# One core, a gated mix of a state-space convolution and segmented attention: reciprocals, softmax sums, joined rows and results moved by fewer, larger DMAs, partial results stored to the output and read back there

## The chip, the cores and the metric

The kernel runs on one core of a Trainium2 chip. The metric is the device time of one execution in microseconds; the chip is not shared with another kernel. A core has a matrix engine (PE, with its weight loads PEld), a vector engine (DVE), a scalar engine (ACT), a general one (POOL), and SyncE (SP), which computes nothing and issues nearly all DMAs of this kernel. The transfers themselves are carried by the core's 16 DMA engines.

## The reference

The input is `x` of 2048 rows and 448 columns. Two branches are computed from it and mixed by a gate, one number per row:

```
g   = sigmoid((x * gate_w).sum(-1))
a   = conv(x, K) + x * D_skip            # K from a diagonal state-space model, by FFT of length 4096
q,k,v = x@wq, x@wk, x@wv                 # 16 heads of 28, four segments of 512 rows
for s in range(4):
    p     = softmax(q_s k_s^T * scale + causal mask)
    a_dot = p @ v_s
    a_mem = (phi(q_s) @ M) / (phi(q_s) @ z + 1e-6)    # M, z: sums over the segments before
    o_s   = sig(beta) * a_mem + (1 - sig(beta)) * a_dot
b   = o @ wo
out = g * a + (1 - g) * b
```

## The kernel before, in words

Everything runs in float32. The first half of the program (to about 440 us) builds the convolution kernel `K` with exponentials and sines, projects `x` to queries, keys and values, and stores what the second half needs in DRAM tiles. The second half interleaves two streams: the attention of 16 units (4 segments by 4 groups of 4 heads; head j of a group holds the partitions 32j to 32j+31) and the convolution by FFT. The order of the work in it is a string, `PLAN`, in which each letter is one step; `run` maps letters to steps. Within an engine the work then stands as the string gives it; DMAs on SP stand in the order in which the scheduler placed them, and SP works through them in that order: a DMA that has to wait holds back those behind it.

The change touches these steps.

- `inverse`, called by `norm` (softmax sums) and by `recall` (sums of the memory branch). The sums of one segment, 4 groups by 512 rows for each of 4 heads, lie as a tile of 128 partitions by 64 columns, 32 partitions for each head. DVE takes the reciprocal `rc` and splits it in two parts `rs[:, 0]` and `rs[:, 1]`, and SP brings each part back as rows of `r8`, one row (one partition) per head: a row of 2048 numbers is gathered from 32 partitions of 64. PE then spreads such rows over the partitions by a matmul with `sel` (`ps_m<-r,sel` in the profile).
- `norm` first brings the sums out of row 28 of each head's 32 partitions of `pvs` into that 128 by 64 tile, `dn`. `norm` and `recall` run once for each of segments 0 to 2 (letter `e`); the last segment divides on PE and DVE instead (`divide`, letter `d`).
- The end of each segment writes `TB`, a DRAM tile of 2048 by 448: for segments 0 to 2 the finished attention part and the skip part, for segment 3 the skip part alone.
- `finish` is the end of the convolution, in 8 steps `wc`. Letter `l` is its `load` (transformed rows `bt`, 896 KB), letter `j` its `join` (the rows of `TB` that belong to the step, into the tile `rest`, of which there are six), letter `z` its `last`: matmuls with `fc` into `py`, a multiply-add of `py` by the gate into `rest` on DVE, and the stores. A tile of step `wc` holds the rows 32n + 16h + 2wc and the next one, for n from 0 to 63 and h of 0 or 1; h picks the half of the partitions. Its rows of segments 0 to 2 (n under 48) are results and go to `out`; those of segment 3 (n from 48) still lack the attention part and go to a DRAM tile `YD`.
- `last_end` reads `YD` back as four tiles `yd`, adds the attention part of segment 3 on DVE, and stores them to `out`, two by SP and two by ACT.

Of the kernel before, what the change touches and what calls it, by code (L numbers as in the profile page):

```python
# [12 lines left out]
F32 = mybir.dt.float32  # L13
# [10 lines left out]
D = 448  # L24
# [3 lines left out]
SEG = 512  # L28
# [442 lines left out]
class Feed:  # L471
# [9 lines left out]
    def step(self):  # L481
        tag = next(self.steps, None)
        self.count += 1
        self.done, self.held = tag is None, tag == "pe"
        cost = tag if isinstance(tag, float) else 0.0
        self.ends = cost < 0
        return abs(cost)
# [165 lines left out]
def finish(nc, k, fp):  # L653

    bv = k.BB.rearrange("k r (h w) d -> (k r) h w d", h=2)
    ov = k.out.rearrange("(n h w) d -> h n w d", h=2, w=16)
    tv = k.TB.rearrange("(n h w) d -> h n w d", h=2, w=16)  # L660
    yv = k.YD.rearrange("(n h w) d -> h n w d", h=2, w=16)
    bts, rest = {}, {}

    def load(wc):
        bts[wc] = fp.tile([128, 2, 2, D], F32, tag="bt", name="bt", bufs=5)
        k.dma(bts[wc], bv[:, :, 2 * wc : 2 * wc + 2])

    def join(wc):
        rest[wc] = fp.tile([128, 2, D], F32, tag="rest", name="rest", bufs=6)
        for h in range(2):  # L670
            k.dma(rest[wc][64 * h : 64 * h + 64], tv[h, :, 2 * wc : 2 * wc + 2])

    def last(wc):
        ws = slice(2 * wc, 2 * wc + 2)
        py = k.ps(("c", "mx")[wc % 2])
        for w in range(2):
            for h in range(2):
                k.mm(
                    py[64 * h : 64 * h + 64, w, :D], k.fc, bts[wc][:, h, w],
                    start=True, stop=True, tile_position=(0, 64 * h),  # L680
                )
        yo = rest.pop(wc)
        for w in range(2):
            i = 2 * wc + w
            k.dve.scalar_tensor_tensor(yo[:, w], py[:, w, :D], k.gt2[:, i : i + 1], yo[:, w], ALU.mult, ALU.add)
        for h in range(2):
            k.dma(yv[h, :, ws], yo[64 * h + 48 : 64 * h + 64])
        for h in range(2):
            k.dma(ov[h, :48, ws], yo[64 * h : 64 * h + 48])

    return load, join, last


# [278 lines left out]
def attend(nc, k, ap):  # L972
# [121 lines left out]
    def inverse(x, rows, dst):  # L1094


        rc = ap.tile([128, 64], F32, tag="rc", name="rc", bufs=2)
        rs = ap.tile([128, 2, 64], F32R, tag="rs", name="rs", bufs=2)
        v.reciprocal(rc, x)
        v.tensor_copy(rs[:, 0], rc)  # L1100
        v.tensor_tensor(rs[:, 1], rc, rs[:, 0], ALU.subtract)
        for b in range(2):
            for j in range(4):
                o = rows + 4 * b + j
                k.dma(
                    dst[o : o + 1].rearrange("o h (i f) -> o (h i) f", f=64).bitcast(F32),
                    rs[32 * j : 32 * j + 32, b].bitcast(F32),
                )

    am, r8 = {}, {}  # L1110

    def recall(s):

        dn = ap.tile([128, 64], F32, tag="dm", name="dm", bufs=1)
        k.ldma(dn, k.DM[s - 1].rearrange("j h (i f) -> (j h i) f", f=64))
        yield
        v.tensor_scalar(dn, dn, 1e-6, None, ALU.add)
        inverse(dn, 32, r8[s - 1])
        yield
        am[s] = ap.tile([128, 4, SEG], F32, tag="am", name="am", bufs=1)  # L1120
        k.ldma(am[s], k.AM[:, :, s - 1].rearrange("h p q -> p h q"))
        yield
        for hg in range(4):
            pb = k.ps("m")
            k.mm(pb, k.sel[32:40], r8[s - 1][32:40, hg], start=True, stop=True)
            v.scalar_tensor_tensor(am[s][:, hg], am[s][:, hg], k.gh[:, hg : hg + 1], pb, ALU.mult, ALU.mult)
            yield

    def norm(s):

        pvs = pvss[s]
        dn = ap.tile([128, 64], F32, tag="dn", name="dn", bufs=1)
        for j in range(4):
            k.dma(
                dn[32 * j : 32 * j + 32],
                pvs[32 * j + 28 : 32 * j + 29].rearrange("o h q -> o (h q)").rearrange("o (i f) -> o i f", f=64),
            )
        r8[s] = ap.tile([40, 4, SEG], F32R, tag="r8", name="r8", bufs=1)
        yield
        inverse(dn, 0, r8[s])  # L1140
        yield
        for hg in range(4):
            o = pvs[:, hg]
            pb = k.ps("m")
            k.mm(pb, k.sel[0:8], r8[s][0:8, hg], start=True, stop=True)
            v.scalar_tensor_tensor(o, o, k.omg[:, hg : hg + 1], pb, ALU.mult, ALU.mult)
            if s > 0:
                v.tensor_tensor(o, o, am[s][:, hg], ALU.add)
            yield
# [30 lines left out]
    def out_mm(s, t, po, hgs):  # L1180
        for hg in hgs:
            k.mm(
                po, pvss[s][:, hg, 128 * t : 128 * t + 128], wo[:, hg],
                start=(hg == 0), stop=(hg == 3),
            )
# [32 lines left out]
    def divide(hg):  # L1218

        o = pvss[3][:, hg]  # L1220
        pb = k.ps("m")
        k.mm(pb, k.den, o, start=True, stop=True)
        rc = ap.tile([128, SEG], F32, tag="jk", name="rcb", bufs=2)
        x = None
        for h in range(2):
            c = slice(256 * h, 256 * h + 256)
            with k.issue_after(x.ins) if x else ExitStack():
                v.reciprocal(rc[:, c], pb[:, c])
            v.scalar_tensor_tensor(o[:, c], o[:, c], k.omg[:, hg : hg + 1], rc[:, c], ALU.mult, ALU.mult)
            x = v.tensor_tensor(o[:, c], o[:, c], am[3][:, hg, c], ALU.add)  # L1230

    def last_end(step, vals):

        s = 3
        yds, pos = [], []
        for t in range(4):
            yd = ap.tile([128, D], F32, tag="xt", name="yd", bufs=4)
            k.dma(yd, k.YD[128 * t : 128 * t + 128])
            yds.append(yd)
        for t in ("w", "mx"):  # L1240
            pt = k.ps(t)
            pos += [pt[:, 0, :D], pt[:, 1, :D]]

        def project(h, hgs):
            for t in (2 * h, 2 * h + 1):
                out_mm(s, t, pos[t], hgs)

        project(0, range(2))
        step(vals)
        project(0, [2])  # L1250
        divide(3)
        project(1, range(2))
        for h in range(2):
            project(h, [2, 3] if h else [3])
            for t in (2 * h, 2 * h + 1):
                po, yd, i = pos[t], yds[t], 12 + t
                v.scalar_tensor_tensor(yd, po, k.ogt[:, i : i + 1], yd, ALU.mult, ALU.add)
                (k.dma, k.adma)[t % 2](k.out[128 * i : 128 * i + 128], yd)

    k.load_wo = load_wo  # L1260
    k.load, k.maxima, k.weigh, k.values, k.seg_end = load, maxima, weigh, values, seg_end
    k.divide, k.last_end, k.skip_last = divide, last_end, skip_last


def second_half(nc, k, ap, tp, fp, fin):
# [55 lines left out]
    def run(c):  # L1321
# [20 lines left out]
        elif c == "v":  # L1342
            step(vals)
        elif c == "q":
            k.twin = False
            k.load(n)
        elif c == "e":
            ends.append(k.seg_end(n))
        elif c == "s":
            while ends and not step(ends[0]):  # L1350
                ends.pop(0)
        elif c == "d":
            k.divide(n)
        elif c == "c":
            step(cv)
        elif c == "C":
            for _ in cv:
                pass
        elif c == "f":
            late = finish(nc, k, fin())  # L1360
        elif c == "k":
            if n == 0:
                skips = k.skip_last()
            else:
                step(skips)
        elif c == "o":
            k.load_wo()
        elif c in "ljz":
            late["ljz".index(c)](n)
# [24 lines left out]
def gated_mix(ctx, tc, k):  # L1394
# [102 lines left out]
    dr = ctx.enter_context(tc.tile_pool(name="dr", bufs=1, space=DRAM))  # L1497
# [11 lines left out]
    k.dr = dr  # L1509
    k.GD = dr.tile([L], F32, name="GD")  # L1510
    k.TB = dr.tile([L, D], F32, name="TB")
    k.YD = dr.tile([SEG, D], F32, name="YD")

    def const(name, ap, shape, dt=F32):
        t = cp.tile(shape, dt, name=name)
# [61 lines left out]
    with ExitStack() as st:  # L1577
# [25 lines left out]
        with ExitStack() as s2:  # L1603
# [5 lines left out]
            n = next(params)  # L1609
            k.ct = gp.tile([128, 2, 512], BF16, name="ct")  # L1610
            constants()
            while n is not None:
# [10 lines left out]
                n = next(params, None)  # L1623
# [68 lines left out]
```

## Time and profile before

| | |
|---|---|
| median of 3 runs | 797.93 us (796.94 to 803.42) |
| the profiled execution's own time | 796.75 us |
| its span, first to last instruction | 795.0 us |
| mean granted PE clock | 0.957 |
| busy share PE / DVE / ACT / POOL | 87% / 73% / 63% / 20% |
| DMA packets, bytes | 96146, 158.70 MB |

A row of the chain of waits has a start and a duration in us and what the chain went through: an engine's work on a tile with its line, a DMA from its issue to its landing (`DMA r<-rs`), or SP's issuing of DMAs (`SPq`). A row of a tile's view has the shortest, median and longest duration in ns, and the first and last start. A row of the table by stretches has the stretch, the busy time of PE, PEld, DVE, ACT and POOL with the count of instructions, the granted PE clock, the mean busy share of the 16 DMA engines, and the GB/s that they moved.

### The profile page before, as it was taken

The numbers are of one execution on the slowest core, as the hardware profiler recorded it, in microseconds if no ns is written. First come the engines' busy times: TensorE is split into PE (matmuls) and PEld (weight loads), VectorE is DVE, ScalarE is ACT, GpSimd is POOL, SyncE is SP. The second block draws the span as 40 slices with busy tenths as digits, with TensorE's granted clock in tenths as the row PEclk, the third lists the DMA queues.
The fourth block names the chain that finished last, engine by engine and source line by source line (L and its number), as shares of the span: only waits on it lengthen the run. The fifth ranks groups of instructions, "written<-read, shape, count | busy, mean of one in ns | idle before, by whom it ended". The sixth has DMA issues, their size and how long they took to land.

```text
span 795.0 us, 19029 instructions
## 1 busy us (share of the span) xinstructions
PE 689.2 (87%) x7609; PEld 382.2 (48%) x7640; DVE 582.7 (73%) x1154; ACT 501.9 (63%) x611; POOL 157.6 (20%) x193
## 2 busy tenths in 40 slices
PE   1676997999888998889997889899998999888987
PEld 1353565666545665447654434444444444444333
DVE  8979689869988798888876775658556757652673
ACT  4877689879998899988984225555345434511320
POOL 4405310111011101110111012232114113410110
PEclk9789999899999999999999999999998999969999
DMA  8628874136453344733357898895959596653973
GB/s 211 170 64 247 252 237 150 43 106 197 153 181 108 106 141 153 227 129 101 128 193 259 325 368 224 299 313 155 368 178 328 158 343 219 214 192 146 269 223 110
DMA packets 96146, 158.70 MB, mean 200 GB/s; under 512 B 25554, under 2 KB 63626, under 8 KB 96058
## 3 DMA queue, kind: packets, MB, share of 16 engines
q1 hardware_dynamic: 92106, 154.78, 59.9%
q10 hardware_dynamic: 3072, 1.84, 0.8%
q8 instruction: 60, 0.98, 0.5%
q0 software_dynamic: 880, 0.87, 0.4%
q14 instruction: 28, 0.23, 0.1%
HBM read 89.25 MB, written 60.24 MB: 188 GB/s over the span
## 4 chain that ended last, share of the span: by engine, by line
PE 51%; DVE 16%; ACT 13%; DMA 12%; issue 5%; SPq 3%; DVEq 0%; ACTq 0%
PE ps_m L1450 18%; PE ps_c L1450 6%; PE ps_w L1450 6%; PE ps_arg L1450 6%; ACT cs L1404 5%; PE ps_pv L1450 5%; PE ps_k L1450 5%; PE ps_mx L1450 4%; DVE Y L401 3%; DVE jk L1404 2%; PE ps_m L1453 2%; DVE cs L381 2%; DVE X L397 2%; DVE Y L402 2%; SPq L1466 1%
## 5 line engine op out<-in xcount | busy, mean ns | idle before, releaser
L1404 ACT ACTIVATE PT<-ps_w 128x1024 f32<-128x1024 f32 (+1 forms) x96 | 84.6, 881 | 127.5 <-PE ps_w L1450 124.3
L1404 DVE CUSTOM_DVE_ANT_0 jk<-ps_mx,mk 128x128 f32<-128x128 f32 (+3 forms) x242 | 106.9, 488 | 59.5 <-PE ps_mx L1450 55.5
L358 POOL TENSOR_TENSOR EX<-EX,cab 128x1024 f32<-128x1024 f32 x28 | 53.5, 1912 | 292.8 <-ACT EX L1404 209.1
L1404 ACT ACTIVATE cs<-ps_arg 128x1024 f32<-128x1024 f32 x97 | 94.5, 1023 | 11.0 <-DVE cs L381 10.8
L1071 POOL TENSOR_SCALAR_AFFINE_SELECT PT<-PT 128x256 f32<-128x256 f32 (+1 forms) x96 | 46.9, 488 | 235.2 <-ACT PT L1404 232.7
L1450 PE MATMUL ps_w<-qu,ku 32*128 32x512 f32 (+3 forms) x768 | 88.0, 347 | 3.0 <-ACT PT L1404 2.5
L1450 PE MATMUL ps_m<-xh,w 128*128 128x512 f32 x224 | 79.1, 413 | 1.5 <-DMA w<-WD 1.5
L1450 PE MATMUL ps_k<-Y,X 128*32 128x64 f32 x3584 | 62.9, 223 | 15.4 <-DVE Y L402 14.9
L397 DVE TENSOR_TENSOR X<-EX,cs 128x1024 f32<-128x1024 f32 x56 | 69.3, 1237 | 6.2 <-ACT cs L1404 5.6
L1450 PEld LDWEIGHTS ps_k<-Y,X 128*32 128x32 f32 x3584 | 53.6, 111 | 41.3 <-DVE Y L402 29.2
L1450 PEld LDWEIGHTS ps_w<-qu,ku 32*128 32x128 f32 x768 | 61.2, 189 | 23.6 <-ACT PT L1404 12.2
L401 DVE TENSOR_TENSOR Y<-EY,cs 128x1024 f32<-128x1024 f32 x56 | 70.1, 1252 | 0.0
L1404 ACT ACTIVATE cs<-cs,bhp 128x1024 f32<-128x1024 f32 x56 | 64.3, 1149 | 1.4
L1404 ACT ACTIVATE EY<-ps_arg 128x1024 f32<-128x1024 f32 x52 | 52.2, 1037 | 4.0 <-PE ps_arg L1450 3.8
L1450 PE MATMUL ps_mx<-ku,qu 32*128 32x128 f32 (+3 forms) x242 | 43.1, 389 | 12.2 <-DVE mx L1404 10.4
L1450 PEld LDWEIGHTS ps_m<-xh,w 128*128 128x128 f32 x224 | 42.0, 188 | 18.9 <-issue 8.9
L403 DVE SCALAR_TENSOR_TENSOR Y<-EY,cs 128x512 f32<-128x512 f32 x56 | 39.0, 696 | 15.3 <-ACT cs L1404 14.2
L1450 PE MATMUL ps_m<-xl,w 128*128 128x512 f32 x128 | 50.1, 391 | 0.0
L1450 PE MATMUL ps_arg<-ct,lh 64*128 64x512 bf16 x224 | 44.3, 382 | 4.7 <-ACT cs L1404 3.1
L1450 PEld LDWEIGHTS ps_mx<-ku,qu 32*128 32x128 f32 x242 | 21.0, 187 | 52.1 <-DVE mx L1404 29.7
L1450 PEld LDWEIGHTS <-lh 64*128 64x128 bf16 x392 | 22.0, 94 | 49.8 <-issue 35.1
L1450 PE MATMUL ps_m<-wo,pvs 128*128 128x448 f32 x96 | 40.9, 571 | 1.1 <-DVE tb L1404 1.1
(220 smaller groups left out, 1313.9 us busy)
## 6 DMA issues: line engine op xcount, KB each, us to landing
w<-WD SPq DMA_DIRECT2D x32, 448.0 KB
qu<-QD SPq DMA_DIRECT2D x16, 512.0 KB
ku<-KD SPq DMA_DIRECT2D x16, 512.0 KB
GU<-gs SPq DMA_DIRECT2D x32, 224.0 KB
GK<-gs SPq DMA_DIRECT2D x8, 896.0 KB
gk<-GK SPq DMA_DIRECT2D x16, 448.0 KB
gu<-GU SPq DMA_DIRECT2D x16, 448.0 KB
ks<-ks SPq DMA_DIRECT2D x32, 224.0 KB
```

Source lines behind the costliest of these rows:

```text
L358: nc.gpsimd.tensor_tensor(o, o, cab, ALU.mult)
L381: v.tensor_scalar(t[:, 0].rearrange("p w t c -> p t w c").bitcast(I32), pv.bitcast(I32), 0x7FFFFFFF, None, ALU.bitwise_and)
L397: v.tensor_tensor(X, ex, t[:, :, 0], ALU.mult)
L401: v.tensor_tensor(Y[:, :, :, :32], lo, y[:, :, :, ::-1], ALU.mult)
L402: v.tensor_tensor(Y[:, 0, :, 32:], ey[:, :, 32:], y[:, 0], ALU.mult)
L403: v.scalar_tensor_tensor(Y[:, 1, :, 32:], ey[:, :, 32:], -1.0, y[:, 1], ALU.mult, ALU.mult)
L1071: nc.gpsimd.affine_select(sl, sl, pat, ALU.is_ge, 0.0, base=0, channel_multiplier=-1)
L1404: x = op(*args, **kw)
L1450: tc.keep_in_program_order(nc.tensor.matmul(*args, **kw))
L1453: tc.keep_in_program_order(nc.tensor.transpose(*args))
L1466: return nc.sync.dma_start(*args)
```

## The change

The four DMAs of a part of the reciprocals become one, and so do the four that bring the sums out of `pvs`; the two halves of a join become one DMA, and the four stores of a `last` (two to `YD`, two to `out`) become one store of the whole tile to `out`, results and unfinished rows alike. `last_end` reads the unfinished rows from `out`. `YD` is gone. The bytes that move are the same.

```
     def join(wc):
         rest[wc] = fp.tile([128, 2, D], F32, tag="rest", name="rest", bufs=6)
-        for h in range(2):
-            k.dma(rest[wc][64 * h : 64 * h + 64], tv[h, :, 2 * wc : 2 * wc + 2])
+        k.dma(rest[wc], tv[:, :, 2 * wc : 2 * wc + 2])
...
     def last(wc):
...
-        for h in range(2):
-            k.dma(yv[h, :, ws], yo[64 * h + 48 : 64 * h + 64])
-        for h in range(2):
-            k.dma(ov[h, :48, ws], yo[64 * h : 64 * h + 48])
+        k.dma(ov[:, :, ws], yo)
...
     def inverse(x, rows, dst):
...
         for b in range(2):
-            for j in range(4):
-                o = rows + 4 * b + j
-                k.dma(
-                    dst[o : o + 1].rearrange("o h (i f) -> o (h i) f", f=64).bitcast(F32),
-                    rs[32 * j : 32 * j + 32, b].bitcast(F32),
-                )
+            o = rows + 4 * b
+            k.dma(
+                dst[o : o + 4].rearrange("o h (i f) -> o (h i) f", f=64).bitcast(F32),
+                rs[:, b].bitcast(F32),
+            )
...
     def norm(s):
...
-        for j in range(4):
-            k.dma(
-                dn[32 * j : 32 * j + 32],
-                pvs[32 * j + 28 : 32 * j + 29].rearrange("o h q -> o (h q)").rearrange("o (i f) -> o i f", f=64),
-            )
+        k.dma(
+            dn,
+            pvs.rearrange("(j e) h q -> j e (h q)", e=32)[:, 28].rearrange("j (i f) -> j i f", f=64),
+        )
...
     def last_end(step, vals):
...
-            k.dma(yd, k.YD[128 * t : 128 * t + 128])
+            k.dma(yd, k.out[128 * (12 + t) : 128 * (12 + t) + 128])
```

`tv` and `ov` are views of `TB` and `out` as `h n w d`, with h of length 2 outermost.

On SP, the end of segment 2 stands so before the change (a row has the line, the transfer as destination and source, the shape of the destination as the built program carries it, outermost length first, and the count of such DMAs in a row):

```order
L1466 DMA V<-VD 128x4x512
L1466 DMA dn<-pvs 32x1x64 x4
L1466 DMA BB<-bs 128x2x448 x2
L1466 DMA r_8596<-rs 1x32x64 x16
L1466 DMA bt<-BB 128x2x896 x5
L1466 DMA am<-AM 128x4x512
L1466 DMA TB<-tb 128x448 x4
```

and so with it (the number in `r` is that of its buffer):

```order
L1459 DMA V<-VD 128x4x512
L1459 DMA dn<-pvs 128x1x64
L1459 DMA BB<-bs 128x2x448 x2
L1459 DMA r_8562<-rs 4x32x64 x2
L1459 DMA bt<-BB 128x2x896 x5
L1459 DMA r_8562<-rs 4x32x64 x2
L1459 DMA am<-AM 128x4x512
L1459 DMA TB<-tb 128x448 x4
```

Sixteen issues of reciprocals became four, and the second two, those of the memory branch, now stand behind the five loads of `bt`.

The joins and the last stores follow on SP. Before:

```order
L1466 DMA rest<-TB 64x896 x12
L1466 DMA bt<-BB 128x2x896
L1466 DMA YD<-rest 16x896 x2
L1466 DMA out<-rest 48x896 x2
L1466 DMA bt<-BB 128x2x896
L1466 DMA YD<-rest 16x896 x2
L1466 DMA out<-rest 48x896 x2
L1466 DMA rest<-TB 64x896 x2
```

and with the change, to the end of the program:

```order
L1459 DMA rest<-TB 128x1x896 x6
L1459 DMA bt<-BB 128x2x896
L1459 DMA out<-rest 2x64x896
L1459 DMA bt<-BB 128x2x896
L1459 DMA out<-rest 2x64x896
L1459 DMA rest<-TB 128x1x896
L1459 DMA bt<-BB 128x2x896
L1459 DMA out<-rest 2x64x896
L1459 DMA rest<-TB 128x1x896
L1459 DMA out<-rest 2x64x896 x5
L1459 DMA yd<-out 128x448 x4
L1459 DMA out<-yd 128x448 x2
```

The order of joins, loads and stores is the same, with one DMA where two or four stood. The DRAM side of a join, which these rows do not show, has the shape of `tv[:, :, 2 * wc : 2 * wc + 2]`, 2x64x896, like that of a store. The four `yd` wait for all eight stores to `out`, as they waited for all the stores to `YD`.

More of the change, by code (lines that the diff above doesn't have):

```diff
@@ L660, in finish @@
     tv = k.TB.rearrange("(n h w) d -> h n w d", h=2, w=16)
-    yv = k.YD.rearrange("(n h w) d -> h n w d", h=2, w=16)
     bts, rest = {}, {}
@@ L1511, in gated_mix @@
     k.TB = dr.tile([L, D], F32, name="TB")
-    k.YD = dr.tile([SEG, D], F32, name="YD")
     def const(name, ap, shape, dt=F32):
```

## The prediction

> **What bounds the kernel now.** I read the page first: the engines' shares, then the share of the chain that ended last, then DMA.
>
> ```profile
> span 795.0 us, 19029 instructions
> PE 689.2 (87%) x7609; PEld 382.2 (48%) x7640; DVE 582.7 (73%) x1154; ACT 501.9 (63%) x611; POOL 157.6 (20%) x193
> ...
> PE 51%; DVE 16%; ACT 13%; DMA 12%; issue 5%; SPq 3%; DVEq 0%; ACTq 0%
> ```
>
> PE works for most of the span and holds half of the chain, so the kernel as a whole is bound by PE. But DMAs and SP's issuing (SPq) stand on the chain for 15%, some 120 us, and the change touches nothing but DMAs. So the question is which of them it touches, and whether they are among those 15%. The chain in order of time, from 560 us on, answers for the places of the change:
>
> ```profile
> 607.10 0.56 SPq L1466
> 607.71 0.58 SPq L1466
> 608.34 0.58 SPq L1466
> 608.97 4.37 DMA dn<-pvs
> ...
> 667.94 2.99 DMA TB<-xt
> ...
> 697.08 0.28 SPq L1466
> 697.40 0.59 SPq L1466
> 698.04 0.59 SPq L1466
> 698.67 1.90 DMA r<-rs
> ...
> 753.05 4.64 DMA out<-rest
> 757.77 0.45 SPq L1466
> 758.26 0.60 SPq L1466
> 758.90 0.58 SPq L1466
> 759.58 8.27 DMA bt<-BB
> ...
> 790.12 0.68 DVE yd L1404
> ```
>
> Each small DMA holds SP for about 0.6 us, and at 607, 697 and 757 us the end of the program waits for such issues in a row: the sums of a segment, its reciprocals, and a `bt` load that stands behind joins and stores. These waits are what fewer DMAs take away. The bytes are the other half of the question. What the DMA engines do at the end of the program stands in the table by stretches:
>
> ```profile
> core 0: us, PE busy (x) PEld busy (x) DVE busy (x) ACT busy (x) POOL busy (x), PEclk, DMA share, GB/s
> 708.50:716.00 7.50, 7.28 (x28) 3.95 (x29) 4.25 (x12) 1.02 (x1) 0.41 (x1) 0.50 1.03 412
> 745.00:760.00 15.00, 14.24 (x99) 5.64 (x99) 13.79 (x20) 4.87 (x6) 2.22 (x4) 1.00 0.99 297
> ```
>
> Where loads of `bt` follow each other, all 16 engines are busy (share 1.03) and move 412 GB/s, that is **25.75 GB/s for one engine**. From 745 to 760 us, in the midst of the stores, they are as busy and move 297 GB/s, 18.6 for each. This stage has no spare DMA time: what takes longer here is late.
>
> **The change, part by part.** First the issues. These are the groups that change:
>
> ```profile
> L1466 SPq DMA_DIRECT2D r<-rs x48: 502/588/1113, 538.4 to 703.7; - x48
> L1466 SPq DMA_DIRECT2D dn<-pvs x12: 562/589/1277, 525.2 to 683.9; - x12
> L1466 SPq DMA_DIRECT2D rest<-TB x16: 450/595/605, 735.4 to 758.3; - x16
> L1466 SPq DMA_DIRECT2D YD<-rest x16: 314/484/1269, 748.2 to 773.8; - x16
> L1466 SPq DMA_DIRECT2D out<-rest x16: 320/420/1481, 749.0 to 774.7; - x16
> ```
>
> The 48 become 12 and the 12 become 3: 45 issues less at 0.59 us, 26.5 us of SP's time over three segment ends. Of this only what the chain shows pays. At 607 us three issues of `dn` go, 1.7 us. Near 698 us, eight issues become two ahead of the first matmul with `r`; the chain has 1.5 us of issues there, and the second of two would go out some 3 us earlier than the eighth, so 1.5 to 3. I take **6 us earlier** at the first join, with another 1 to 2 for loads that stood behind the sixteen issues. The ends are 0 and 12 us: nothing if another wait is as late, and twice the sum if the first two segment ends give as much as the last. Against it, the second pair of reciprocals now stands behind five `bt` loads, 4.59 MB or 11 us at 412 GB/s; PE needs them only after the four `TB` stores, more than 30 us later in the trace before, so I cost it at nothing. A merged small transfer may land later than the four it replaces; the nearest rows are 1.90 us for `r` and 4.37 for `dn`, so nothing to 2.5 us, inside the same ends.
>
> Now the joins and stores: 16 issues become 8 and 32 become 8. In bytes, a whole join or store is 128 rows of 3584 bytes, 458,752 in all. On 16 engines it takes 458,752 / 412,000 = 1.1 us. But the trace of before has no large transfer with an outermost length under 16: the halves carried 64, 48 and 16 rows outermost, and the merged ones carry 2 on the DRAM side (2x64x896). Over how many engines such a transfer is dealt is the unknown on which all rests. The nearest row is `DM<-am`, which stores 4 rows of 2 KB. In a stretch with little else, 203 to 206 us, the DMA view gives:
>
> ```profile
> DMA packets 152, 0.27 MB, mean 90 GB/s; under 512 B 20, under 2 KB 20, under 8 KB 152
> ...
> AM<-am SPq DMA_DIRECT2D x1, 256.0 KB
> DM<-am SPq DMA_DIRECT2D x1, 8.0 KB
> ```
>
> `AM` has 128 rows of 2 KB and `DM` 4: 132 packets of data. The other 20 are too small for data; they are closing packets, one from each engine that carried a share. 16 for `AM` leave 4 for `DM`: an outermost length of 4 ran on four engines. It does not prove the rule, since 4 rows fill no more than four engines anyhow. The bounds are therefore 16 engines (nothing lost) and 2 (eight times as long), and I take **2**, the reading by which each of these transfers, `DM` too, is dealt by whole slices of its outermost length.
>
> The Trainium skill, page "DMA: Bandwidth & Descriptors", section on why a DMA increments its semaphore by 16, says the same as a rule: a DMA runs on the largest number of engines up to 16 that divides the slowest length other than 1 on both sides. By this rule 128 against 2 gives 2 engines, and 128 against 4 (the merged `r` and `dn`) gives 4; the four closing packets of `DM` agree, and no row here shows a pair of unequal lengths.
>
> On two engines a transfer takes 229,376 bytes / 25.75 GB/s = **8.9 us**, and there are 16 of them on the same two. The sum for these two engines, which work through what SP gave them in order:
>
> ```profile
> L1404 DVE SCALAR_TENSOR_TENSOR rest<-ps_mx,gt,rest x8: 669/676/684, 748.1 to 771.6; 128x448 f32<-128x448 f32 x8
> ...
> L1404 DVE SCALAR_TENSOR_TENSOR yd<-ps_w,ogt,yd x2: 672/674/675, 787.4 to 788.0; 128x448 f32<-128x448 f32 x2
> L1404 DVE SCALAR_TENSOR_TENSOR yd<-ps_mx,ogt,yd x2: 673/678/683, 790.1 to 790.7; 128x448 f32<-128x448 f32 x2
> ```
>
> - First join issued at 735.4 before, now 6 us earlier: 729.4. First bytes at the latest 1.9 us on (`r<-rs`): 731.3.
> - Six joins, then three `bt`, eight stores and two joins as SP has them. Joins 7 and 8 wait for the stores that free their tiles, but those stores are queued on the two engines by then, with a store and a `bt` behind them: no gap. 16 x 8.9 = 142.4 us, and three `bt` of 917,504 bytes on 16 engines, 2.2 us each: 6.7. The last store ends at 880.4.
> - `yd` can be read only then: a load of 224 KB, 3.0 us as `TB<-xt` took: 883.4.
> - Four multiply-adds of 0.68 us, 2.7: 886.1. Before, the last of them ended at 790.7 + 0.7 = 791.4 and the span at 795.0: 3.6 us for the store and the end: 889.7.
>
> The rest of the work is not later: its last join is the eleventh of the sixteen transfers (eight joins, three stores), so ready at about 731.3 + 11 x 8.9 + 6.7 = 836. Before, 15.8 us lay between the last multiply-add of `rest` (771.6) and the first of `yd` (787.4); 836 + 1 + 16 is 30 us ahead of `yd`. PE, DVE and ACT stall in this stage and none of them sets the end. The read-back itself adds no wait of a new kind, since `yd` waited for the `YD` stores too.
>
> The profiled execution took 796.75 us, 1.75 more than its span, and lies 1.2 below the median shown. 889.7 + 1.75 = 891.5, so I say **892 us**, 12% over.
>
> **The rivals.** (1) *All 16 engines carry the merged transfers*, because the SBUF side has 128 partitions and these decide. Place: joins and stores; it decides as soon as a store takes 1.1 us instead of 8.9. For it: the halves ran well, and every transfer with 128 partitions in the trace did. Against: the DRAM side carries 2 outermost, as the built program has it. Then 6 us are saved ahead, and at 757 us the three issues before the `bt` load shrink to one, 1.2 us, and of the four before it two go, 1 us: 796.75 - 8 = **788 us**. With the gain ahead at its lower end it is 795, no change.
>
> The Trainium skill, same page, rules for kernel authors, leads there: many small transfers are to be merged, and two transfers to halves of the partitions replaced by one over 128, since both halves use all the engines anyhow. By this rule alone the change would pay; the trace agrees on the price of an issue (0.59 us) and has no merged one.
>
> (2) *One side decides, so that only the joins or only the stores run on two engines.* Eight transfers: stores alone start near 742 and end at 742 + 8 x 8.9 + 6.7 = 820, plus 3.0 + 2.7 + 3.6 + 1.75 gives 831; joins alone end at 731.3 + 71.2 + 6.7 + 8 x 1.1 = 818, and the 15.8 us, the four multiply-adds and 3.6 follow: 842. Between them **837 us**. Against it: no row asks for two kinds of transfers.
>
> (3) *Two engines, but at the rate of the stage with stores*, 18.6 GB/s each: 12.3 us a transfer, 16 x 3.4 = 55 more: **947 us**. For it: the row of 745 to 760 us. Against: those engines were shared by loads and stores of all kinds, while here fourteen of sixteen lie still.
>
> **How the numbers follow.** Forecast 0.80, rival 1 0.09 (0.07 faster by over 1%, 0.02 within), rival 2 0.05, rival 3 0.06. 1% is about what a measurement of this kernel can tell from no change. The range takes in the gain ahead at both ends (-6 and +6), a rate for one engine up to a fifth better than the row (16 x 1.5 = 24 less), and most of rival 3 on the upper side: 865 to 940. Slower has 0.80 + 0.05 + 0.06 = 0.91.
>
> **What would show it.** Right: in the changed kernel, eight `out<-rest` and eight `rest<-TB`, a long stretch from about 745 to 880 us with a DMA share near 2/16 and 50 GB/s, the chain there held by `rest<-TB` and `out<-rest`, `yd` late by some 100 us, and PE with long idle times there. The first join some 6 us earlier shows the gain at the segment ends. Wrong: a DMA share as before in that stage (rival 1), joins that land in 2 to 3 us beside stores that take 9 (rival 2). The prediction fails most simply if the outermost length does not deal the transfers out.

## The result: 11.5% slower, and the profile after

The changed kernel takes 893.82 us (median of four, 890.06 to 895.45) against 800.67 for the kernel before; the ratio is 1.1152, with a 95% interval from 1.1071 to 1.1233. The prediction said 892 us. The profiled execution took 893.21 us, its span is 891.5 us. The page shows nearly the same work in a longer span (shares of the span by engine, then the chain that ended last, by engine and by line):

```profile
span 891.5 us, 18960 instructions
PE 703.1 (79%) x7640; PEld 383.4 (43%) x7640; DVE 582.6 (65%) x1154; ACT 501.4 (56%) x611; POOL 158.3 (18%) x193
...
PE 43%; DVE 18%; DMA 17%; ACT 7%; issue 4%; SPq 3%; DVEq 0%; POOL 0%; ACTq 0%; POOLq 0%
PE ps_m L1443 16%; DMA rest<-TB 7%; DMA out<-rest 7%; PE ps_c L1443 6%; PE ps_arg L1443 4%; PE ps_pv L1443 4%; PE ps_w L1443 4%; PE ps_k L1443 4%; ACT cs L1397 3%; DVE Y L401 3%; PE ps_mx L1443 3%; SPq L1459 3%; DVE jk L1397 2%; DVE X L397 2%; DVE Y L402 2%
```

DVE, ACT and POOL are as busy as before to within 1 us and PE to within 14; the 96 us more are in the main waiting. Two kinds of DMAs that were small on the chain, the joins and the stores, now hold 7% each, 118 us together in the rows below. The chain in order of time shows where:

```profile
727.43 1.95 DMA TB<-tb
...
730.71 7.38 SPq L1459
...
738.14 30.35 DMA rest<-TB
...
774.78 1.26 SPq L1459
776.08 9.77 SPq L1459
...
785.96 23.51 DMA out<-rest
...
809.53 29.45 DMA rest<-TB
...
847.79 34.74 DMA out<-rest
...
882.69 0.34 SPq L1459
883.08 0.42 SPq L1459
883.54 3.62 DMA yd<-out
887.26 0.68 DVE yd L1397
```

From the first join to the read-back the chain holds joins, stores, SP's issuing (9.77 us of it for a `bt` load, at 776.08) and some multiply-adds on DVE, which are left out here. A join or store takes up to 35 us from issue to landing, since it stands behind others. Loads of `bt` are late too, off this chain: from 735 us on PE waits 36 us for two of them, which SP issued late (last section). What the DMA engines do meanwhile is in the table by stretches (columns as before; the last two are the DMA share and GB/s) and, for the first stretch, in the DMA view:

```profile
748.00:758.00 10.00, 6.19 (x16) 2.05 (x16) 1.93 (x3) 0.00 (x0) 0.00 (x0) 0.51 0.13 51
820.00:835.00 15.00, 12.82 (x44) 5.55 (x48) 5.64 (x7) 1.19 (x2) 1.28 (x2) 0.57 0.13 53
865.00:873.00 8.00, 0.00 (x0) 0.00 (x0) 0.00 (x0) 0.00 (x0) 0.00 (x0) 0.50 0.13 53
```

```profile
DMA packets 144, 0.51 MB, mean 51 GB/s; under 512 B 2, under 2 KB 2, under 8 KB 144
...
rest<-TB SPq DMA_DIRECT2D x2, 448.0 KB
```

A share of 0.13 is two of 16 engines, 51 to 53 GB/s is 25.5 to 26.5 for each, and where a join ends there are two closing packets, not 16. In the last of the three stretches nothing computes at all: the kernel waits for two DMA engines.

### The profile page after: what moved, and what is told of

Its sections match the earlier page's. It is cut to its first block, busy times and chain, and to the rows that moved or that the text cites. A ratio compares the mean times of both kernels' runs of the same rounds, so it can differ in the third digit from the quotient of the medians.

```text
span 891.5 us, 18960 instructions
## 1 busy us (share of the span) xinstructions
PE 703.1 (79%) x7640; PEld 383.4 (43%) x7640; DVE 582.6 (65%) x1154; ACT 501.4 (56%) x611; POOL 158.3 (18%) x193
## 4 chain that ended last, share of the span: by engine, by line
PE 43%; DVE 18%; DMA 17%; ACT 7%; issue 4%; SPq 3%; DVEq 0%; POOL 0%; ACTq 0%; POOLq 0%
PE ps_m L1443 16%; DMA rest<-TB 7%; DMA out<-rest 7%; PE ps_c L1443 6%; PE ps_arg L1443 4%; PE ps_pv L1443 4%; PE ps_w L1443 4%; PE ps_k L1443 4%; ACT cs L1397 3%; DVE Y L401 3%; PE ps_mx L1443 3%; SPq L1459 3%; DVE jk L1397 2%; DVE X L397 2%; DVE Y L402 2%
## 5 line engine op out<-in xcount | busy, mean ns | idle before, releaser
L1443 PE MATMUL ps_mx<-bt,fc 128*64 128x448 f32 x32 | 11.5, 862 | 42.9 <-DMA bt<-BB 36.1
L1443 PE MATMUL ps_pv<-wz 128*128 128x512 bf16 x143 | 43.4, 394 | 0.5
```

The source lines that it names most:

```text
L1443: tc.keep_in_program_order(nc.tensor.matmul(*args, **kw))
```

## Experiments

Each run is compared with runs of the kernel before on the same chip; ratios are to those.

**The theory**: a transfer is dealt over as many engines as the lengths of its outermost dimension on both sides allow, so that 2 on one side means two engines. The main rivals: the reading back of the output, and something about the merged form itself (its issue on SP, or its unequal sides).

**Halves again (e1).** The changed kernel, with joins and stores cut at the half of the partitions; everything else of the change stays, the read-back from `out` too.

```
-        k.dma(rest[wc], tv[:, :, 2 * wc : 2 * wc + 2])
+        for h in range(2):
+            k.dma(rest[wc][64 * h : 64 * h + 64], tv[h, :, 2 * wc : 2 * wc + 2])
...
-        k.dma(ov[:, :, ws], yo)
+        for h in range(2):
+            k.dma(ov[h, :, ws], yo[64 * h : 64 * h + 64])
```

> The changed kernel with joins and stores cut into their two halves again (64 rows outermost on both sides); reciprocals and sums stay merged, results and unfinished rows go to out in the same two stores, and are read back from out. Theory (two engines carry whatever has 2 outermost): the tail is as before, 796.75 less some 6 us ahead of the joins less 1 to 3 us for 16 stores less = about 788 us, at most 795. Rival A (reading the output back and waiting for whole stores is what costs): stays near 890. Rival B (the merged small transfers on four engines cost time): 797 or more.

Measured: 786.49 us (785.41 to 792.82) against 798.07, ratio 0.9865 (0.9816 to 0.9913). All of the loss goes. The median is the lowest of all the kernels, though the runs overlap with those of e2 and e8 below. The read-back is not what costs (rival A falls): the `yd` rows of this run, loads on SP and then the multiply-adds on DVE, are

```profile
L1461 SPq DMA_DIRECT2D yd<-out x4: 343/427/430, 770.3 to 771.7; - x4
L1399 DVE SCALAR_TENSOR_TENSOR yd<-ps_w,ogt,yd x2: 674/676/677, 777.7 to 778.3; 128x448 f32<-128x448 f32 x2
```

The loads are out 6 us ahead of the first multiply-add. In the changed kernel's chain above, a multiply-add of `yd`, the third of the four, starts as its `yd` lands.

**Only the small transfers (e2, e8, e9).** The kernel before with the merged `inverse` and `norm` (e2); with the merged `inverse` alone (e8); with the merged `norm` alone (e9). The edits are the parts of the diff for these functions.

> The kernel before with only the reciprocals and the softmax sums merged; joins, stores and YD as before. Theory: the issues that go pay some 6 us at the segment ends, 791 us, first join issued at 729 to 730 us instead of 735.4. Rival B: the small transfers land later on four engines, and the second pair of reciprocals stands behind the loads of bt: no gain, 797 or more.

> The kernel before with only the reciprocals merged (48 issues become 12). By the prediction's split of the gain ahead of the joins, 1.5 to 3 us near 697 us and 1 to 2 us for loads behind the sixteen issues: first join issued 3 to 5 us earlier than 735.4. If instead the order of SP's queue matters more than these issues, up to 12 us or none.

> The kernel before with only the softmax sums merged (12 issues become 3). By the prediction's split, 1.7 us at 607 us: first join issued 1 to 2 us earlier than 735.4. If the merged transfer on four engines lands later than the four it replaces, nothing or later.

Measured: e2 790.13 us (six runs, 786.39 to 793.07) against 798.07, ratio 0.9879 (0.9837 to 0.9920). e8 790.72 (two runs, 788.37 to 793.08) against 799.66, 0.9878 (0.9789 to 0.9968). e9 796.83 (eight runs, 790.92 to 801.14) against 799.66, 0.9961 (0.9917 to 1.0004): no change that can be told. The first join starts as follows (rows of the tile `rest` for e2, e8 and e9 in this order):

```profile
L1464 SPq DMA_DIRECT2D rest<-TB x16: 450/595/597, 728.3 to 751.2; - x16
```

```profile
L1465 SPq DMA_DIRECT2D rest<-TB x16: 450/594/597, 729.9 to 752.8; - x16
```

```profile
L1465 SPq DMA_DIRECT2D rest<-TB x16: 450/595/600, 732.2 to 755.0; - x16
```

That is 7.1, 5.5 and 3.2 us before the 735.4 of the kernel before. So fewer issues do pay, and rival B falls. By the medians most of it comes from the reciprocals, though the two runs of e8 overlap with those of e9. How well these places are known: up to the joins, e1, e6, e7 and the changed kernel issue the same DMAs, and their first joins start at 730.2, 733.8, 724.8 and 729.5. A single profile tells such a gain to some 4 or 5 us only, and what e9 gains in its profile its times do not show.

Steadier than these places are two distances in the last segment end: from DVE's reciprocal of the softmax sums (`rc<-dn`) to PE's first matmul with `r`, and from there to the first join. The first is 8.0 us in the kernel before and in e9, and 5.9 to 6.0 in the changed kernel, e1, e2, e6, e7 and e8. So 2 us are gained there by fewer issues of reciprocals: in the kernel before and in e9 PE stands idle for 2.2 us until `r` lands, and in the others it does not wait for it. The second distance holds more: 34.5 us before and 31.5 in e9, against 28.3 to 28.4 in the six others. Two rows of the chain and one of the table by stretches show why, first for the kernel before, then for the changed one (the third number from the end of a stretch is the granted clock):

```profile
700.81 0.76 PE ps_m L1450
...
713.89 4.69 PE ps_m L1450 x8
```

```profile
705.00:717.00 12.00, 11.72 (x43) 5.96 (x41) 5.73 (x14) 2.05 (x2) 0.80 (x2) 0.50 0.95 356
```

```profile
701.15 0.49 PE ps_m L1443
...
709.65 3.29 PE ps_m L1443 x8
```

```profile
700.00:710.00 10.00, 8.63 (x55) 4.06 (x54) 8.81 (x28) 3.15 (x4) 2.32 (x4) 1.00 1.01 397
```

The first matmul with `r` starts no earlier than before. But behind it the granted clock of PE is 0.50 in the kernel before, for some 16 us, and the same eight matmuls take 4.69 us in place of 3.29. In e9 the clock is 0.50 for some 10 us, from 703 on. In all the kernels with merged reciprocals it is 1.00 there. So most of what the small transfers gain ahead of the joins in these profiles lies where the clock was low before: 6 us. Whether PE's wait for `r` brings the low clock on was not tried: each kernel has one profile, and the clock falls for a while at other places in kernels of both kinds (a mean of 0.89 from 610 to 640 us in the kernel before, e1, e2, e8 and e9). In the profile of e9 merging the sums gains nothing ahead of the reciprocal, 692.7 against 692.9 us; its 3.2 us lie where the clock was low for a shorter time.

**The rule: quarters cut at 62, 57 and 48 (e3, e4, e5).** As e1, with each half cut once more, so that each DMA has one row length on both sides and the same bytes move:

```
         for h in range(2):
-            k.dma(ov[h, :, ws], yo[64 * h : 64 * h + 64])
+            for x in (slice(0, 62), slice(62, 64)):
+                k.dma(ov[h, x, ws], yo[64 * h + x.start : 64 * h + x.stop])
```

and likewise for the joins; 57 and 48 in place of 62 for e4 and e5.

> As e1, but each half of a join or store cut into DMAs of 62 and 2 rows, each with one row length on both sides. Theory (largest divisor up to 16 of the outermost length): 62 and 2 both give two engines, each carries 64 rows of a transfer as in the changed kernel, so the same 8.9 us for each of 16 transfers and about 893 us. Rival C (at most 16 engines, as many as there are rows): 62 rows go to 16 engines, about 790 to 800 us. Rival D (SP needs 8.9 us to issue a DMA whose two sides have different shapes, and the engines wait for SP): these have equal shapes, so 790 to 800 us too.

> As e3, cut at 57 and 7 rows. Theory: 57 rows give three engines with 19 rows each, 7 rows seven engines with one each; the first three carry 40 rows of a transfer, 40 x 0.139 = 5.6 us, 16 of them and three bt 96 us from 732 on, then 9 us as in the changed kernel's end: about 839 us. Rival C and D: 790 to 800 us, as for e3.

> Control for e3 and e4: the same 64 joins and stores in quarters, cut at 48 and 16 rows, both of which sixteen divides. Theory: 16 engines for each, so the number of DMAs costs only SP's issues; 32 issues more than e1 in the tail, at 0.4 to 0.6 us, partly on the chain: 787 to 797 us. If quartering itself had cost what e3 and e4 showed, this is 840 to 890 us.

| cut | engines, by the largest divisor up to 16 | expected us | measured us | ratio |
|---|---|---|---|---|
| 62 and 2 | 2 and 2 | 893 | 893.97 (892.85 to 895.10) | 1.1184 (1.1113 to 1.1256) |
| 57 and 7 | 3 and 7 | 839 | 840.99 (838.05 to 843.92) | 1.0521 (1.0449 to 1.0594) |
| 48 and 16 | 16 and 16 | 787 to 797 | 793.39 (786.62 to 796.84) | 0.9891 (0.9803 to 0.9980) |

Sixty-two rows, with equal and simple shapes on both sides, run as slowly as the merged transfers; 48 run as fast as 64 within the noise (e1 has a ratio of 0.9865). Neither the count of DMAs, nor unequal sides, nor the number of rows explains that; a divisor does. The stretches by DMA share show the engines, first 62, then 57:

```profile
836.00:846.00 10.00, 4.19 (x14) 1.56 (x14) 1.28 (x2) 0.60 (x1) 0.00 (x0) 0.50 0.13 52
```

```profile
816.00:826.00 10.00, 8.52 (x22) 3.62 (x20) 5.25 (x6) 0.00 (x0) 0.00 (x0) 1.00 0.20 80
```

Two engines at 52 GB/s, three (and a little of four more) at 80: 26 and some 27 GB/s each, within a tenth of the 25.75 that one engine moved before.

**One side at a time (e6, e7).** The changed kernel with only the stores in halves (e6), or only the joins (e7).

> The changed kernel with only the stores cut into halves; the joins stay whole. Theory: eight joins of 9.1 us on two engines from 732 on, with three bt and a sixteenth of each store among them: last join about 820, then 15.8 + 2.7 + 3.6 us of work: 844 us. By the rule on both sides it must be about as slow as e7; if the destination's shape alone decides (128 here), 787 us.

> The changed kernel with only the joins cut into halves; the stores stay whole. Theory: eight stores of 8.7 us on two engines from about 743 on, with three bt and the joins' shares among them: last store about 821, then 9 us as at the changed kernel's end: 832 us. If the source's shape alone decides (128 here), 787 us.

Measured: e6 839.68 us (837.16 to 842.20) against 800.18, ratio 1.0477 (1.0381 to 1.0573); e7 830.47 (829.67 to 831.27), ratio 1.0362 (1.0274 to 1.0451). Both come out near what the expectations say for eight transfers on two engines, 844 and 832 us. In a join the 2 is on the source's side, in a store on the destination's, so either side is enough. The stretches, e6 in its joins, then e7 in its stores:

```profile
748.00:770.00 22.00, 11.32 (x50) 3.36 (x50) 3.21 (x5) 1.62 (x2) 1.04 (x2) 0.69 0.13 52
```

```profile
770.00:815.00 45.00, 17.23 (x75) 7.82 (x76) 6.52 (x8) 1.28 (x3) 1.27 (x2) 0.76 0.13 53
```

In e7 the way was as expected too: the last store lands at 818.8 us, where 821 was said. In e6 it was not: the last join is used at 810.6 us already, where 820 was said, and the chain then goes through a `bt` load that SP held back (797.2 to 812.2) and PE's work behind it. The two losses, 39.5 and 30.3 us, sum to less than the 93 of the changed kernel. Part of that is the base: all three kernels hold the merged small transfers, so e1 is what they are to be compared with. Against its ratio of 0.9865 the losses are 0.061 and 0.050, together 0.111, and that of the changed kernel is 0.129; some 14 us are left. Why these do not add up was not tried; each of the two alone may overlap with work on PE and DVE that is left in the tail.

## Why the prediction was right, step by step

- **First join 6 us earlier, at 729.4**: 729.5, but the sum behind it was not right, and that the number agrees to 0.1 us is luck; the kernels with the same DMAs up to there spread over 9 us. Of its terms, the 1.5 to 3 us at the reciprocals are shown: 2.0, from 8.0 to 6.0. The 1.7 us at the sums are not: where the chain before waited for `dn` until 613.3 us, that of the changed kernel waits for loads of `ks` and `cf` until 612.9, e9 gains nothing ahead of the reciprocal, and in the changed kernel's profile DVE starts it 2.3 us later than before (695.2 against 692.9). In place of the 1 to 2 us for loads behind the sixteen issues, 6.2 us were gained from the first matmul with `r` to the first join, where the granted clock no longer fell to 0.50. The prediction's row of 708.5 to 716 us has this clock, and only its DMA columns were read. Together: 6.2 and 2.0 less 2.3, 5.9. The second pair of reciprocals, behind five `bt` loads, cost nothing, as said: PE has no wait for it in that segment end.
- **Two engines**: shown by the share of 0.13 and the two closing packets, by e3 against e5, and for each side by e6 and e7. The rule of the Trainium skill (page "DMA: Bandwidth & Descriptors", section on why a DMA increments its semaphore by 16), the largest number up to 16 that divides both lengths, agrees with each of these runs: 2 and 128, 62, 57, 48 and 64.
- **8.9 us a transfer at 25.75 GB/s**: 51 to 53 GB/s for the two, 8.7 to 9.0 us. In e3, where each engine has the same rows, the medians, 893.97 and 893.82 us, agree better than the runs of either.
- **The last store at 880.4**: it landed at 847.79 + 34.74 = 882.5, 2 us late over 150. The working said that no gap opens while SP waits for the stores that free tiles. That holds for the engines, but not for SP, which was held by its own issues (below): `bt` and the first store went out at 765 and 774 us, not in the 740s. It cost little, presumably because what SP held back for these two engines would have stood in their queue anyhow.
- **The end**: first multiply-add of `yd` at 885.2 against 883.4 forecast, span 891.5 against 889.7. Nearly all of this is the late last store: the first multiply-add came 2.7 us after it, where 3.0 was said. The load in the chain above took 3.6 us.
- **The rest of the work not late**: right. PE, DVE and ACT wait in this stage, and the last join (838.98 in the chain, where 836 was said) left them 46 us until `yd`.
- **Rivals.** (1), all 16 engines, falls; its time of 788 us was that of e1 (786.5), which is the same kernel with transfers that do run on 16. So the advice to merge halves into one transfer over 128 partitions (rules for kernel authors, the same page of the Trainium skill) did not hold here: the halves lost no time, and the merged transfer ran on two engines. (2) fell for the change as made, but e6 and e7 are its two halves, forecast at 842 and 831 and measured at 839.7 and 830.5. (3), a lower rate for each engine, fell: alone, two engines moved 25.5 to 26.5 GB/s each, against 18.6 for each in the busy stage before.

## What to carry to other kernels

Before two DMAs are merged, look at the outermost length that each side of the merged one has in the built program: it should be divisible by 16, or the transfer loses engines (2, 57 and 62 did here, 48 and 64 did not), and the cheapest check afterwards is the DMA share of the stage (0.13 is two engines of 16). For small transfers fewer engines may cost nothing: 48 DMAs of 8 KB made into 12 paid 1.2% (0.3 to 2.1%) here, in the profiles where a wait of PE went and with it a stretch of low clock. For large ones two DMAs of 64 rows beat one of 2 by 64 rows, with joins and stores together 786 us against 894, and a read-back through the output costs nothing where the stores have landed by then.

## What was not expected of the hardware

SP is held when transfers queue on few engines. These are the joins in the changed kernel (shortest, median, longest issue in ns):

```profile
L1459 SPq DMA_DIRECT2D rest<-TB x8: 503/7777/8875, 729.5 to 809.5; - x8
L1459 SPq DMA_DIRECT2D out<-rest x8: 542/6173/14293, 773.9 to 847.8; - x8
```

The first two joins were issued in 0.56 and 0.53 us, the third held SP for 7.38, and the next for 8.87, the time in which the two engines carry one transfer. With some 128 rows waiting on an engine (two transfers of 64 rows for each), SP went on only as fast as the engines did, and every DMA behind was held too, the `bt` loads among them, which use the idle engines as well. Where the limit lies and whether it counts rows was not tried.
